# One-sided expert blocks of a mixture-of-experts kernel: the last weight chunk's low part is cast later, and the next block's column groups are turned in another order

## The chip, the cores and the metric

The kernel runs on one core of one Trainium2 chip. The metric is device time in microseconds (us) of one execution; three executions of the kernel before are shown. The core's engines are TensorE (PE; its weight loads are listed as PEld), VectorE (DVE), ScalarE (ACT), GpSimd (POOL) and SyncE (SP), and each runs its own list of instructions in order. They meet only where one waits for a count that another has reached.

## What is computed

Three stages on 1792 rows of width 768, in fp32:

```python
scores = scale * np.matmul(q, k.transpose(0, 1, 3, 2)) - np.log(S)   # 4 x 12 heads, 448 x 64
x = np.matmul(1.0 / (1.0 + np.exp(-scores)), v)                      # then one row per token, 768 wide

do_compute = x @ w_skip > 0                      # the other tokens keep x
e_idx = np.argmax(xc @ w_gate, axis=1)           # top-1 of 8 experts, xc = x[do_compute]
h = np.maximum(xc[mask] @ w1[e], 0.0)            # 768 -> 1024
out[do_compute] = xc + gate_w * (h @ w2[e])      # 1024 -> 768

h = out @ w_in                                   # dense, 768 -> 2048
g = np.where(h > 0.0, h, np.exp(np.minimum(h, 0.0)) - 1.0)
return g @ w_out                                 # 2048 -> 768
```

## The kernel before, in words

A product of two fp32 arrays is made of three matmuls on halves of the numbers: high by high, high by low, low by high (lines 556 to 558, `gemm`). So whatever enters a matmul is first cast to its **high part** by ACT and then has its **low part** (the value less its high part) made by DVE.

**Stages.** Attention comes first, then the experts, then the dense network. The change lies in the experts' stage, which ends 425.6 us after the start of the profiled span.

**Blocks.** The tokens that are not skipped are sorted by expert into blocks of 256 slots, two halves of 128 rows each; a block belongs to one expert. How many tokens an expert has is known only on the chip, so `level(i, k)` (line 1218) is a nest of branches that picks for block i one of several arms: both halves full, one half and a few rows, or the **one-sided arm**, one half only, `expert(i, k, (P,))`. In this run blocks 5, 6 and 7 are one-sided: they take 347 to 367.4, 367.4 to 388 and 388 to 408.4 us. There is no block 8 to compute; in its place `close(8)` and `after_close()` run, from 408.4 to 425.6 us, and turn the first rows of the dense stage.

**A one-sided block.** A block has 8 weight chunks of 128 x 1536, numbers 0 to 3 of w1 and 4 to 7 of w2. `split_w` casts a chunk's high part on ACT (line 547, tile `whi`) and makes its low part on DVE (line 549, tile `wlo`); there are 4 buffers of each. `ahead(i, c)` does so two chunks early, so that `ahead(i, 5)` makes the parts of **chunk 7**. In the one-sided arm the order of the program is: chunks 0 to 3 by `up_parts`, which leave h in rows (`hs`) in two halves; the first half of h turned into columns (`h_columns(0)`); `ahead(i, 5)` (line 1026); chunk 4 by `back`; the second half turned, `h_columns(1)`. A turn is four PE transposes (`flip`, line 142) into a PSUM bank, then ACT's relu of the bank to a high part (line 894) and DVE's low part (line 895). `h_columns(1)` uses bank `pt1`.

**Between two blocks.** The next level begins with `between(i)`: `columns(i, ends)` turns the next block's rows `xg` into columns, in three groups; each is four transposes by `flip_rows` (line 142 again) into one of the banks `ends = (pt0, pt1, acc1)`, then a high part by ACT (line 571) and a low part by DVE (line 573). Then come chunks 5 and 6 of the block before (`back`, lines 556 to 558), the branch `two` (line 1229), and chunk 7 of the block before in `lead_in`. `close` and `after_close` do the same at the end, with three more groups into other banks and a branch (line 1223) ahead of chunk 5.

**What sets the order.** Each engine's instructions stand in the order in which the program names them. An instruction that uses a tile waits for the tile's last users on other engines. It does so by a count: each engine counts its instructions up, and the wait names the count of the instruction that it needs. Two arms of one branch end at the same count, so that what follows can wait for a number that holds for both. `acc1`, the third of `ends`, is also the bank of a block's last product in the other two arms, where the last thing that DVE does is to add that product to the rows (`outcome`, line 1052).

Of the kernel before, what the change touches and what calls it, by code (L numbers as in the profile page):

```python
# [91 lines left out]
def build(nc, tc, a):  # L92
# [3 lines left out]
    with ExitStack() as top:  # L96
# [44 lines left out]
        def flip(dst, src):  # L141
            nc.tensor.transpose(dst, src, ident)  # L142
# [34 lines left out]
        with ExitStack() as st:  # L177
# [5 lines left out]
            x2 = both_t[:, : 2 * KD].rearrange("p (s c) n -> p s c n", s=2)  # L183
# [357 lines left out]
            def split_w(i, c, hi=True, lo=True):  # L541
                if i == NB:
                    return
                j = 8 * i + c
                raw, w_hi, w_lo = raw_of(i, c), whi_t[j % NSPL], wlo_t[j % NSPL]
                if hi:
                    nc.scalar.copy(w_hi, raw)  # L547
                if lo:
                    nc.vector.tensor_sub(w_lo, raw, w_hi)  # L549
# [10 lines left out]
            def flip_rows(i, g, pt):  # L560
                for j in range(2):
                    for h in range(2):
                        flip(
                            pt[:, (2 * j + h) * P : (2 * j + h + 1) * P],
                            xg_t[i % NXG][h][:, (2 * g + j) * P : (2 * g + j + 1) * P],
                        )

            def split_columns(g, pt, dst, hi=True, lo=True):
                o, pt = slice(2 * g, 2 * g + 2), pt.rearrange("p (c n) -> p c n", c=2)
                if hi:  # L570
                    nc.scalar.copy(dst[:, 0, o], pt)  # L571
                if lo:
                    nc.vector.tensor_sub(dst[:, 1, o], pt, dst[:, 0, o])  # L573

            def columns(i, banks):
                for g, pt in enumerate(banks):
                    flip_rows(i, g, pt)
                    split_columns(g, pt, x2)

            steps = B * NP  # L580
            raw = load(0, 0, True)
# [129 lines left out]
            ends = (*pt_t, acc_t[1])  # L711
# [167 lines left out]
            def h_columns(nh, sizes):  # L879
                for h, n in enumerate(sizes):  # L880
                    pt = pt_t[(nh + h) % 2].rearrange("p (c n) -> p c n", c=4)[:, :, :n]
                    for j in range(4):
                        w = slice(j * P, (j + 1) * P)
                        if n == P:
                            flip(pt[:, j, :], hs_t[nh][:, w])
                        else:
                            nc.tensor.matmul(
                                pt[:, j, :], hf_t[nh][:, w], fold[:, :n], start=True, stop=True
                            )
                    t = slice(h * P, h * P + n)  # L890
                    h_hi, h_lo = h2[:, nh, 0, :, t], h2[:, nh, 1, :, t]
                    if n < P:
                        h_lo = h2[:, nh, 0, :, h * P + n : (h + 1) * P]
                    nc.scalar.activation(h_hi, pt, AF.Relu)
                    nc.vector.scalar_tensor_tensor(
                        h_lo, pt, 0.0, h_hi, op0=ALU.max, op1=ALU.subtract
                    )
# [23 lines left out]
            def ahead(i, c, **parts):  # L921
                c += 2
                split_w(i + c // 8, c % 8, **parts)
# [87 lines left out]
            def expert(i, k, sizes, following=None):  # L1011
                whole = sizes == (P, P)

                def soon():
                    outcome(i - 1, 0, P)

                if whole:
                    up_two(i, soon)
                    ahead(i, 4)
                else:  # L1020
                    up_parts(i, sizes, soon)
                    if len(sizes) > 1:
                        skips(f"many{i}", 1 - (k >> 1))
                    elif i + 1 < NB:
                        skips(f"more{i + 1}", (following + 3) >> 2)
                ahead(i, 5)
                for h, n in list(enumerate(sizes))[1:]:
                    if whole:
                        back(i, h, n, range(4, 8))
                        outcome(i, h, n)  # L1030
                        back(i, 0, P, range(4, 5))
                    else:
                        back(i, h, n, range(4, 6))
                        h_columns(1, sizes)
                        back(i, h, n, range(6, 8))
                        back(i, 0, P, range(4, 5))
                        outcome(i, h, n)
                if len(sizes) == 1:
                    back(i, 0, P, range(4, 5))
                    h_columns(1, sizes)  # L1040

            def outcome(i, h, n):
                gated(xg_t[i % NXG][h], slot_gate[:, 2 * i + h : 2 * i + h + 1], h, n)
# [41 lines left out]
                    scatter(i - 2)  # L1085

            def between(i):
                columns(i, ends)
                back(i - 1, 0, P, range(5, 7))
                split_w(i, 0)  # L1090
                split_w(i, 1)
# [80 lines left out]
            def close(i):  # L1172
                if i == 1:
                    gather(1)
                s = 2 * (i - 1)
                nc.gpsimd.tensor_copy(last_rows[0], xg_t[(i - 1) % NXG][0])
                nc.gpsimd.tensor_copy(last_gate[0], slot_gate[:, s : s + 1])
                nc.gpsimd.tensor_copy(last_slot[0], slot_tok[:, s : s + 1])
                give(xg_t[(i - 1) % NXG][1], slot_tok[:, s + 1 : s + 2])
                for g in range(3):  # L1180
                    flip_rows(i, g, ends[g])
                for g in range(3):
                    flip_rows(i + 1, g, later[g])

            def after_close():

                for g in range(3):
                    split_columns(g, ends[g], x2)
                back(0, 0, P, range(5, 6))
                for g in range(3):  # L1190
                    split_columns(g, later[g], xd[:, 1], lo=g == 0)
                back(0, 0, P, range(6, 8))
                gated(last_rows[0], last_gate[0], 0, P)
                give(last_rows[0], last_slot[0])
                for g in range(1, 3):
                    split_columns(g, later[g], xd[:, 1], hi=False)
                xh, xl = x_dense
                terms = [(w[:, cc], xh[:, cc]) for w in wi0 for cc in range(KD)]
                terms += [(wi0[0][:, cc], xl[:, cc]) for cc in range(KD)]
                for k_, (w, x) in enumerate(terms):  # L1200
                    nc.tensor.matmul(  # L1201
                        acc_t[1], w, x, start=(k_ == 0), stop=(k_ == len(terms) - 1)
                    )
# [47 lines left out]
        with ExitStack() as st:  # L1251
# [156 lines left out]
            for s, (bi, f) in enumerate(steps):  # L1408
# [12 lines left out]
                g = curve(nt * P, ph)  # L1421
# [53 lines left out]
```

## Time and profile before

| | before |
|---|---|
| median of 3 executions | 904.13 us (903.27 to 906.42) |
| the profiled execution | 903.78 us |
| its span in the profile | 902.0 us |
| granted TensorE clock | 1.000 |
| PE busy | 880.9 us, 98% |
| DVE busy | 557.5 us, 62% |
| ACT busy | 485.5 us, 54% |

The profile shows one execution; its own time stands 0.35 us under the median, and the span 1.8 us under that, for what lies around it. Times in the trace count from the start of the span. A row of the timeline gives a start, a length and an instruction (or several alike in a row), and behind it in brackets how long the engine had been idle and on what it had waited. Matmuls overlap: one starts before the one ahead of it has ended.

### The profile page before, as it was taken

How to read it: one execution, taken by the hardware profiler on the slowest of the kernel's cores; microseconds unless marked ns; L12 is line 12 of the kernel's file. 1: busy time of each engine (PE TensorE's matmuls, PEld its weight loads, DVE VectorE, ACT ScalarE, POOL GpSimd, SP SyncE). 2: the span in 40 equal slices, each digit the busy share in tenths (PEclk: the TensorE clock that was granted, in tenths of full speed). 3: DMA queues.
4: the chain of work that ended last, by engine and by line, in shares of the span. 5: the costliest groups of instructions: out<-in, count | busy, mean ns of one | idle time of the engine just before them, and what ended most of it. 6: DMA issues, size and time to landing. Idle time of an engine off the chain costs nothing.

```text
span 902.0 us, 13626 instructions
## 1 busy us (share of the span) xinstructions
PE 880.9 (98%) x5208; PEld 710.4 (79%) x5208; DVE 557.5 (62%) x872; ACT 485.5 (54%) x680; POOL 80.8 (9%) x79
## 2 busy tenths in 40 slices
PE   9999999999999898998999999999999999999998
PEld 4445545699999787887888888888888888888997
DVE  2968778697666465885888886444344444344664
ACT  7777776554455464773645554434444434344664
POOL 1000000112101022332100000100000100000100
PEclk9999999999999999999999999999999999999999
DMA  8788875779956175955733430100000100000100
GB/s 291 260 281 274 302 262 200 262 276 405 373 181 232 45 293 202 410 215 197 242 96 102 123 105 19 70 1 18 18 18 19 70 1 1 1 1 18 53 1 36
DMA packets 34194, 134.71 MB, mean 149 GB/s; under 512 B 4698, under 2 KB 5850, under 8 KB 34098
## 3 DMA queue, kind: packets, MB, share of 16 engines
q1 hardware_dynamic: 29474, 114.22, 35.6%
q0 software_dynamic: 4480, 19.01, 5.9%
q8 instruction: 56, 0.92, 0.4%
q14 instruction: 40, 0.33, 0.1%
q10 hardware_dynamic: 144, 0.23, 0.1%
HBM read 112.47 MB, written 23.99 MB: 151 GB/s over the span
## 4 chain that ended last, share of the span: by engine, by line
PE 54%; issue 0%; DVE 0%; ACT 0%; ACTq 0%
PE acc L1350 16%; PE pt L1350 10%; PE acc L1318 9%; PE acc L1319 9%; PE acc L1317 8%; PE acc L142 1%; PE acc L1201 0%; PE acc L556 0%; PE acc L557 0%; PE acc L558 0%; DVE both L573 0%; ACT both L571 0%; ACT raw L1361 0%; ACTq L1471 0%; ACTq L571 0%
## 5 line engine op out<-in xcount | busy, mean ns | idle before, releaser
L549 DVE TENSOR_TENSOR wlo<-raw,whi 128x1536 fp32r<-128x1536 f32 x64 | 111.7, 1763 | 28.4 <-ACT whi L547 27.0
L1328 DVE SCALAR_TENSOR_TENSOR m<-m,acc 128x512 f32<-128x512 f32 (+1 forms) x64 | 39.7, 620 | 139.4 <-ACT m L1327 139.4
L1326 ACT ACTIVATE m<-acc 128x512 f32<-128x512 f32 (+1 forms) x64 | 34.9, 545 | 167.9 <-PE acc L1319 158.4
L547 ACT CAST whi<-raw 128x1536 fp32r<-128x1536 f32 x64 | 93.9, 1483 | 17.3 <-PE acc L558 6.6
L249 ACT ACTIVATE at<-ps,bias 112x896 f32<-112x896 f32 x96 | 88.9, 1010 | 23.3 <-PE ps L242 23.0
L1350 PE MATMUL acc<-wol,gh 128*128 128x256 f32 x320 | 100.8, 315 | 0.0
L1350 PE MATMUL acc<-woh,gl 128*128 128x256 f32 x320 | 100.4, 314 | 0.0
L1350 PE MATMUL acc<-woh,gh 128*128 128x256 f32 x320 | 100.4, 314 | 0.0
L1318 PE MATMUL acc<-x,wih 128*128 128x512 f32 (+1 forms) x270 | 96.2, 356 | 0.0
L1317 PE MATMUL acc<-x,wih 128*128 128x512 f32 (+1 forms) x270 | 96.2, 356 | 0.0
L1319 PE MATMUL acc<-x,wil 128*128 128x512 f32 (+1 forms) x270 | 96.1, 356 | 0.0
L556 PE MATMUL acc<-whi,both 128*128 128x384 f32 (+1 forms) x236 | 83.9, 355 | 2.7 <-DVE both L573 1.6
L557 PE MATMUL acc<-wlo,both 128*128 128x384 f32 (+1 forms) x236 | 82.9, 351 | 0.6 <-DVE wlo L549 0.6
L558 PE MATMUL acc<-whi,both 128*128 128x384 f32 (+1 forms) x236 | 82.5, 350 | 0.0
L256 PE MATMUL po<-at,vt 112*64 112x448 f32 x384 | 77.5, 545 | 0.0
L1306 DVE TENSOR_TENSOR wol<-wo,woh 128x768 fp32r<-128x768 f32 x64 | 61.2, 956 | 23.4 <-ACT woh L1305 23.0
L1350 PEld LDWEIGHTS acc<-woh,gh 128*128 128x128 f32 x320 | 60.3, 188 | 9.9
L1350 PEld LDWEIGHTS acc<-wol,gh 128*128 128x128 f32 x320 | 60.3, 188 | 9.5
L1305 ACT CAST woh<-wo 128x768 fp32r<-128x768 f32 x64 | 53.3, 833 | 26.0 <-PE acc L1350 25.9
L1332 DVE TENSOR_TENSOR gl<-m,gh 128x512 fp32r<-128x512 f32 (+1 forms) x64 | 40.0, 626 | 40.5 <-ACT gh L1331 40.5
L1350 PEld LDWEIGHTS acc<-woh,gl 128*128 128x128 f32 x320 | 60.1, 188 | 4.2
L1300 DVE TENSOR_TENSOR wil<-wi,wih 128x768 fp32r<-128x768 f32 x60 | 57.4, 956 | 7.6 <-ACT wih L1299 6.9
(268 smaller groups left out, 1872.2 us busy)
## 6 DMA issues: line engine op xcount, KB each, us to landing
raw<-in_w SPq DMA_DIRECT2D x66, 768.0 KB, 12.4
raw<-in_wi SPq DMA_DIRECT2D x9, 768.0 KB
raw<-in_wo SPq DMA_DIRECT2D x9, 768.0 KB, 7.1
vt<-in_v SPq DMA_DIRECT2D x12, 448.0 KB, 6.4
raw<-in_wi SPq DMA_DIRECT2D x14, 384.0 KB
raw<-in_wo SPq DMA_DIRECT2D x14, 384.0 KB, 3.1
qr<-in_q SPq DMA_DIRECT2D x11, 448.0 KB, 4.3
kr<-in_k SPq DMA_DIRECT2D x11, 448.0 KB, 4.1
```

Of the source, the lines that this page charges most:

```text
L249: nc.scalar.activation(at[:, :, c, :], ps[:CP, :, :S], AF.Sigmoid, bias=bias[:CP], scale=QK_SCALE)
L256: nc.tensor.matmul(po[64 * j : 64 * j + 64, :S], vt[:, 2 * (hp % 2) + j, c, :], at[:, j, c, :], start=(c == 0), stop=(c == NCH - 1),)
L547: nc.scalar.copy(w_hi, raw)
L549: nc.vector.tensor_sub(w_lo, raw, w_hi)
L556: nc.tensor.matmul(o, a_hi, b_hi, start=first, stop=False)
L557: nc.tensor.matmul(o, a_hi, b_lo, start=False, stop=False)
L558: nc.tensor.matmul(o, a_lo, b_hi, start=False, stop=last)
L1306: nc.vector.tensor_sub(pair[1], wo_r[f], pair[0])
L1317: nc.tensor.matmul(o, a, b, start=(cc == 0), stop=False)
L1318: nc.tensor.matmul(o, a, c, start=False, stop=False)
L1319: nc.tensor.matmul(o, wil[:, cc], b, start=False, stop=(cc == KD - 1))
L1350: nc.tensor.matmul(o, a, b, start=(clears and f == 0 and k_ == 0), stop=(f == KF2 - 1 and k_ == 2), skip_group_check=True,)
```

## The change

Two edits, both about the place where a one-sided block passes into the next one.

1. In the one-sided arm `ahead(i, 5)` makes only the high part of chunk 7 at its old place; the low part is made after `h_columns(1)`, so that on DVE it stands behind the low part of h's second half (line 895) and not ahead of it. The other arms keep both parts where they were.
2. `columns` takes an order of the groups, and `between`, `close` and `after_close` turn the groups first, third, second: the banks in the order `pt0`, `acc1`, `pt1`.

```diff
-            def columns(i, banks):
-                for g, pt in enumerate(banks):
-                    flip_rows(i, g, pt)
-                    split_columns(g, pt, x2)
+            def columns(i, banks, turns=(0, 1, 2)):
+                for g in turns:
+                    flip_rows(i, g, banks[g])
+                    split_columns(g, banks[g], x2)
...
-                ahead(i, 5)
+                ahead(i, 5, lo=len(sizes) > 1)
...
                 if len(sizes) == 1:
                     back(i, 0, P, range(4, 5))
                     h_columns(1, sizes)
+                    ahead(i, 5, hi=False)
...
             def between(i):
-                columns(i, ends)
+                columns(i, ends, (0, 2, 1))
...
-                for g in range(3):
+                for g in (0, 2, 1):
                     flip_rows(i, g, ends[g])
...
-                for g in range(3):
+                for g in (0, 2, 1):
                     split_columns(g, ends[g], x2)
```

From line 1039 on, the changed kernel's line numbers are one higher.

**On DVE**, at the end of a one-sided arm and the start of the next block (all these arms read alike): `wlo_1914` and `wlo_1916` are the low parts of chunks 6 and 7, `pt_1902` and `pt_1903` are `pt0` and `pt1`, and what stands in brackets is what the instruction waits for.

```order
 L895 SCALAR_TENSOR_TENSOR both<-pt_1902,both 128x4x128 [waits Activation_49]
 L549 TENSOR_TENSOR wlo_1914<-raw_2325,whi_1913 128x1536 [waits DMAHW2_49,Activation_49]
-L549 TENSOR_TENSOR wlo_1916<-raw_2326,whi_1915 128x1536 [waits DMAHW3_49,PE_49,Activation_49]
-L895 SCALAR_TENSOR_TENSOR both<-pt_1903,both 128x4x128 [waits Activation_49]
-L1229 UNCONDITIONAL_BRANCH
-L1223 COMPARE_AND_BRANCH
+L895 SCALAR_TENSOR_TENSOR both<-pt_1903,both 128x4x128 [waits Activation_49]
+L549 TENSOR_TENSOR wlo_1916<-raw_2326,whi_1915 128x1536 [waits DMAHW3_49,DVE_49]
+L1230 UNCONDITIONAL_BRANCH
+L1224 COMPARE_AND_BRANCH
 L573 TENSOR_TENSOR both<-pt_1902,both 128x512 [waits Activation_49]
```

The low part of chunk 7 and that of h have changed places, and the arm's last DVE instruction is now the former.

**On PE**, the same place in the kernel before: the last turn of h, the jump, and the first transpose into each of the three banks (`acc_1905` is `acc1`; `xg_1921` holds the next block's rows).

```order
L142 MATMUL pt_1903<-cst,hs_2317 128x128 [waits Activation_49]
L1229 UNCONDITIONAL_BRANCH
L1223 COMPARE_AND_BRANCH
L142 MATMUL pt_1902<-cst,xg_1921 128x128 [waits DMASW2_49,DVE_49]
...
L142 MATMUL pt_1903<-cst,xg_1921 128x128 [waits DVE_49]
...
L142 MATMUL acc_1905<-cst,xg_1921 128x128 [waits Activation_49]
...
L556 MATMUL acc_1908<-whi_1834,both 128x384
```

And in the changed kernel:

```order
L142 MATMUL pt_1903<-cst,hs_2317 128x128 [waits Activation_49]
L1230 UNCONDITIONAL_BRANCH
L1224 COMPARE_AND_BRANCH
L142 MATMUL pt_1902<-cst,xg_1921 128x128 [waits DMASW2_49,DVE_49]
...
L142 MATMUL acc_1905<-cst,xg_1921 128x128 [waits DVE_49,Activation_49]
...
L142 MATMUL pt_1903<-cst,xg_1921 128x128
...
L556 MATMUL acc_1908<-whi_1834,both 128x384
```

The transposes into `acc1` now stand second and carry a wait for DVE, and those into `pt1` stand third and carry none. In both built kernels the wait for DVE at this place asks for the count of the arm's last DVE instruction: behind block 5 that is 490, which before is line 895's and in the changed kernel that of chunk 7's low part.

## Rows read from the trace of the kernel before

**Rows 1.** The page: its span and the engines' busy time.

```profile
span 902.0 us, 13626 instructions
PE 880.9 (98%) x5208; PEld 710.4 (79%) x5208; DVE 557.5 (62%) x872; ACT 485.5 (54%) x680; POOL 80.8 (9%) x79
```

**Rows 2.** Windows: from:to and length, each engine's busy time, PE's clock, DMA share, GB/s.

```profile
core 0: us, PE busy (x) PEld busy (x) DVE busy (x) ACT busy (x) POOL busy (x), PEclk, DMA share, GB/s
408.40:425.60 17.20, 14.00 (x85) 12.71 (x84) 8.52 (x12) 4.68 (x9) 4.07 (x4) 1.00 0.67 226
425.60:850.00 424.40, 424.36 (x2210) 360.27 (x2209) 233.65 (x381) 198.66 (x323) 20.17 (x20) 1.00 0.16 53
```

**Rows 3.** Timeline of PE where block 5 passes into block 6.

```profile
start us, us, engine line op out<-in xcount [idle before <-releaser]
367.47 0.60 PE L142 MATMUL pt<-cst,hs 128*128 128x128 f32 x4
367.90 0.60 PE L142 MATMUL pt<-cst,xg 128*128 128x128 f32 x4
370.00 0.66 PE L142 MATMUL pt<-cst,xg 128*128 128x128 f32 x4 [1.50 <-DVE both L895]
370.50 0.60 PE L142 MATMUL acc<-cst,xg 128*128 128x128 f32 x4
370.85 0.42 PE L556 MATMUL acc<-whi,both 128*128 128x384 f32 x1
375.09 0.34 PE L556 MATMUL acc<-whi,both 128*128 128x384 f32 x1
```

**Rows 4.** Timeline of DVE at the same place.

```profile
367.59 1.76 DVE L549 TENSOR_TENSOR wlo<-raw,whi 128x1536 fp32r<-128x1536 f32 x1 [0.32 <-ACT whi L547]
369.26 0.68 DVE L895 SCALAR_TENSOR_TENSOR both<-pt,both 128x512 fp32r<-128x512 f32 x1
369.86 0.68 DVE L573 TENSOR_TENSOR both<-pt,both 128x512 fp32r<-128x512 f32 x1
```

**Rows 5.** Timeline of ACT at the same place.

```profile
366.08 1.48 ACT L547 CAST whi<-raw 128x1536 fp32r<-128x1536 f32 x1
368.11 0.60 ACT L894 ACTIVATE both<-pt 128x512 fp32r<-128x512 f32 x1 [0.55 <-PE pt L142]
368.60 0.58 ACT L571 CAST both<-pt 128x512 fp32r<-128x512 f32 x1
```

**Rows 6.** Timeline of PE behind block 6 (first row) and at the close.

```profile
390.49 0.66 PE L142 MATMUL pt<-cst,xg 128*128 128x128 f32 x4 [1.51 <-DVE both L895]
...
408.44 0.60 PE L142 MATMUL pt<-cst,hs 128*128 128x128 f32 x4
...
411.10 0.66 PE L142 MATMUL pt<-cst,xg 128*128 128x128 f32 x4 [1.63 <-DVE both L895]
411.60 1.91 PE L142 MATMUL acc<-cst,xg 128*128 128x128 f32 x16
415.07 0.41 PE L556 MATMUL acc<-whi,both 128*128 128x384 f32 x1 [1.57 <-DVE both L573]
```

**Rows 7.** Timeline of DVE (both parts in one row), then ACT, at the close.

```profile
406.48 3.96 DVE L549 TENSOR_TENSOR wlo<-raw,whi 128x1536 fp32r<-128x1536 f32 x2
410.37 0.68 DVE L895 SCALAR_TENSOR_TENSOR both<-pt,both 128x512 fp32r<-128x512 f32 x1
...
409.07 0.60 ACT L894 ACTIVATE both<-pt 128x512 fp32r<-128x512 f32 x1 [0.55 <-PE pt L142]
```

**Rows 8.** Timeline of PE and DVE where block 4 passes into block 5.

```profile
347.63 1.09 PE L142 MATMUL pt<-cst,xg 128*128 128x128 f32 x8 [0.98 <-DVE rest L1216]
...
347.42 0.15 DVE L1216 COPY rest<-cst 128x1 f32<-128x1 f32 x1
```

**Rows 9.** Lines 1206 and 1223 by PE's sequencer: count, shortest/median/longest ns, starts.

```profile
L1206 PEldq TENSOR_LOAD <-kinds x1: 307/307/307, 372.0 to 372.0; - x1
...
L1223 PEldq EVENT_SEMAPHORE  x1: 51/51/51, 411.4 to 411.4; - x1
L1223 PEldq COMPARE_BRANCH  x1: 3303/3303/3303, 411.6 to 411.6; - x1
```

**Rows 10.** Line 1229 by PE's sequencer in blocks 5 and 6; PE's timeline in block 5.

```profile
L1229 PEldq COMPARE_BRANCH  x1: 3028/3028/3028, 351.4 to 351.4; - x1
...
L1229 PEldq COMPARE_BRANCH  x1: 447/447/447, 372.4 to 372.4; - x1
...
354.50 0.45 PE L556 MATMUL acc<-whi,both 128*128 128x384 f32 x1 [1.18 <-issue]
```

## The prediction

> **What bounds the kernel now.** I read the page first: PE is busy for 880.9 of 902.0 us [rows 1], so a change counts for as much as it moves PE's idle time, or PE's work. The change has neither more nor fewer instructions of any kind; it can only move idle time. The windows come next: from 425.6 to 850 us PE is busy for 424.36 of 424.40 us [rows 2]. What the experts' stage loses is therefore not made up later: the dense stage has no idle time that could shrink, and a loss passes to the end whole. The window of the close has 17.20 − 14.00 = 3.2 us of idle PE [rows 2].
>
> Then PE's timeline where a one-sided block passes into the next. Behind block 5 it turns h's second half at 367.47, the next block's first group into `pt0` at 367.90, and then stands idle for 1.50 us, till line 895 on DVE has emptied `pt1` [rows 3]. DVE's timeline says why that was late: ACT's relu of `pt1` had ended at 368.11 + 0.60 = 368.71 [rows 5], but DVE was on chunk 7's low part from 367.59, and took line 895 only at 369.26, till 369.94 [rows 4]. PE's idle time ends 0.06 us later, at 370.00. The same is to be seen behind block 6 (1.51 us) and at the close (1.63 us) [rows 6]. These three gaps, 4.6 us together, are all that the change can touch: at the other boundaries no one-sided arm ends.
>
> **What the change aims at.** Line 895 would start when ACT's relu ends, at 368.71 + 0.03 = 368.74 (estimated delay; rows 4 and 5 show no case of their own), and end at 369.42, which is 0.52 us earlier. PE would spend the wait on the transposes into `acc1`. If these need not wait, the gap shrinks.
>
> **What I take them to wait for.** They do wait. The order of the changed kernel shows that the first transpose into `acc1` carries a wait for DVE, where before it had none of its own: it stood behind `pt1`'s, which asked for the same count. That count is the last of the arm, since in the other arms `acc1`'s last reader on DVE is the arm's last instruction, and all arms end at one count. In the kernel before, the one-sided arm's last instruction on DVE is line 895, so that the wait asked for no more than `pt1` needed. In the changed kernel the last is the low part of chunk 7, which no transpose needs. So PE waits in second place for **the very instruction that was moved out of line 895's way**.
>
> Does such a wait for unrelated work bind on the chip? Between blocks 4 and 5 it does: the transposes into `pt0` started at 347.63, idle for 0.98 us, when a DVE copy that only fills up the arm's count (line 1216, which nobody reads) had ended at 347.42 + 0.15 = 347.57 [rows 8].
>
> **The two inner boundaries** (5 to 6, 6 to 7), by block 5's rows. Line 895 runs from 368.74. The next instruction on DVE starts 0.60 us after it, as 369.86 after 369.26 [rows 4]: chunk 7's low part starts at 369.34 and ends, at 1.76 us [rows 4], at 371.10. Its high part was ready at 366.08 + 1.48 = 367.56 [rows 5], so it waits for nothing else. 0.06 us later, at 371.16, PE turns `acc1`'s group, against 370.00 for the first of the two groups before: 1.16 us more idle time. The wait now stands as an instruction of its own in PE's sequencer instead of on the transpose, so the restart has an empty queue; I add an estimated 0.04 us (0 to 0.1). **1.2 us each, 2.4 together** (2.3 to 2.5).
>
> What follows: ACT's cast of `pt0` was done at 368.60 + 0.58 [rows 5] and waits for nobody; DVE's subtraction of it comes 1.2 us later than 369.86 and is needed only by the next block's first chunk, which comes after chunk 7, itself at 375.09 before [rows 3] and now at 376.3. Chunk 7's low part, done at 371.10, is 5 us early for it. So neither ACT nor DVE is late next. The branch between chunks 6 and 7 was met by the sequencer at 372.4 and took 0.45 us [rows 10], 2.2 us ahead of chunk 7: that is the cover, and it stays about as long, as both move. The DMAs and their queues (SP, POOL) keep their places; the low part reads a buffer that is reloaded much later, and 1.2 us do not show there.
>
> **The close** has the same wait and a branch behind it. The relu ends at 409.07 + 0.60 = 409.67 [rows 7]; line 895 would start at 409.70, the low part at 410.30 and end at 412.06, and PE would go on at 412.12 in place of 411.10 [rows 6]: 1.0 us. Then comes what PE's sequencer does. Before, it had handed on 19 transposes during the idle time and came to the branch 0.3 us after the release (its wait at 411.4), and the branch took it 3.303 us [rows 9]: 411.6 + 3.3 = 414.9, and chunk 5 started at 415.07 [rows 6]. So the branch sets chunk 5's start, not the transposes, which ended at 413.5. The changed kernel's sequencer is held at the wait, and then has 20 transposes to hand on before it meets the branch. Behind block 5 it was, at 372.0, past 8 transposes and 24 matmuls [rows 9], when PE had started 8 and 7 of them (24 matmuls from 370.85 to 375.09 [rows 3] are one in 0.177 us): 17 ahead. With 17 ahead it meets the branch when PE begins the fourth transpose, 0.4 us after the release in place of 0.3: the close costs 1.0 + 0.1 = 1.1 us. If it can't get ahead, 20 transposes at 0.12 us each (16 in 1.91 [rows 6]) make 2.4 us: 1.0 + 2.4 − 0.3 = 3.1 us. I take **1.5**, near the lower end, because of the 17.
>
> **The sum.** 1.2 + 1.2 + 1.5 = 3.9 us (2.3 + 1.1 = 3.4 to 2.5 + 3.1 = 5.6). The sum stands against the profiled execution's 903.78 us: 907.7. That execution lies 0.35 us under the median of 904.13, which is well inside the three runs' spread of 3 us. About 0.3% of 904.13, 2.7 us, is what a measurement of this kernel can tell from no change; 3.9 is 0.4%. The case's own range: 906.5 to 909.5.
>
> **Rivals.**
>
> *The wait is over sooner (a gain).* If the transposes into `acc1` are held only until line 895, or not at all, the change does what its parts look like. Not at all: `acc1`'s group fills the idle time and `pt1`'s starts at 369.42 + 0.06 = 369.48, where before the first of the two started at 370.00: with one group done already, PE's next chunk comes 0.52 + 0.35 (a group's time before chunk 5, 370.50 to 370.85 [rows 3]) = 0.87 us earlier; twice, and about 1.0 at the close (1.63 [rows 6] less what is left of it): 2.7 us in all, so 901.1. For it: line 895 does come earlier. Against: the count in the built kernel, and the copy of rows 8. It decides if DVE's count stands otherwise than I read it. 0.05.
>
> *The close hides its share.* If chunk 5's start at 415.07 is set by something that does not move with the wait, only the inner boundaries count: 903.78 + 2.4 = 906.2, within 0.3%. For it: the profile puts that idle time down to line 573 on DVE [rows 6], and the transposes would end at 412.12 + 0.5 + 1.9 = 414.5, still ahead of 415.07. Against: chunk 5 reads nothing of line 573's, and the branch ends 0.16 us ahead of it. The Trainium skill ("Advanced Engine Details and Errata", section "Control Flow Timing") gives a compare-and-branch about 108 ns; by that the branch could not have held chunk 5, and this rival would be the forecast. The 3.303 us of rows 9 speak against it here, thirty times as long. 0.14.
>
> *A slow branch at the inner boundaries too.* In block 5 the branch between chunks 6 and 7 took 3.028 us and left PE idle for 1.18 us [rows 10]; behind it 0.447. With the sequencer held till 371.2 and then 17 ahead, it meets the branch at about 373.2; at 3.03 us it is through at 376.2, and PE's chunk 7, due at 376.3, comes up to 0.4 us later: 3.9 + 2 × 0.4 = 4.7, 908.5. For it: one of three such branches was slow. Against: what is fetched does not change with a microsecond of delay. 0.08.
>
> *Nothing changes*: the waits trade places and times as they were, 903.8 to 904.1. That needs line 895 and the low part to run as before, which their order excludes. 0.03.
>
> **How the numbers follow.** Forecast 0.70, gain 0.05, hidden close 0.14, slow branch 0.08, nothing 0.03. Faster by over 0.3%: the gain case, 0.05 (its 901.1 lies just at that bound; I count it whole). Within 0.3% (up to 906.8): the hidden close, nothing, and some 0.03 of the forecast's lower edge: 0.20. Slower: 0.75. The forecast is 907.7; the range goes down to 905.8, for a hidden close, and up to 909.8, for a close at PE's pace with a little of the slow branch.
>
> **What would show it.** In the changed profile PE's timeline behind blocks 5 and 6 should show one idle time of about 2.7 us (1.50 + 1.2) ahead of the transposes into `acc` rather than `pt`, ended by line 549, not 895, and no idle time ahead of `pt1`'s. On DVE line 895 should start 0.03 us after line 894 ends, and the low part 0.60 us later. At the close the wait of line 1224 should be met at about 412.6 (plus the 2.4 us by which all has moved) and chunk 5 come 3.9 us later than 415.07. I am wrong if the transposes into `acc1` start before the low part ends; if they do wait but chunk 5 at the close comes only 2.4 us later, the second rival holds.

## The result and the profile after

The changed kernel took **911.01 us** in the median of 5 executions (909.07 to 912.09), the kernel before 903.76 (902.89 to 906.42): a ratio of 1.0068, 95% interval [1.0047, 1.0088] (ratios, here and below, are taken over the single executions and need not be the quotient of the medians). It is slower, as forecast, but by about 7 us in place of 3.9, and the median lies outside the range of 905.8 to 909.8. The profiled execution was the fastest of the five, 909.07 us with a span of 907.3; its mean granted clock was 0.995, where that of before was 1.000.

PE's timeline of the changed kernel where block 5 passes into block 6, which answers to [rows 3]:

```profile
367.46 0.60 PE L142 MATMUL pt<-cst,hs 128*128 128x128 f32 x4
367.89 0.60 PE L142 MATMUL pt<-cst,xg 128*128 128x128 f32 x4
371.23 0.63 PE L142 MATMUL acc<-cst,xg 128*128 128x128 f32 x4 [2.73 <-DVE wlo L549]
371.69 0.60 PE L142 MATMUL pt<-cst,xg 128*128 128x128 f32 x4
372.04 0.42 PE L556 MATMUL acc<-whi,both 128*128 128x384 f32 x1
372.30 0.33 PE L557 MATMUL acc<-wlo,both 128*128 128x384 f32 x1
...
372.97 0.52 PE L557 MATMUL acc<-wlo,both 128*128 128x384 f32 x1
373.29 0.52 PE L558 MATMUL acc<-whi,both 128*128 128x384 f32 x1
...
376.46 0.34 PE L557 MATMUL acc<-wlo,both 128*128 128x384 f32 x1
376.64 0.34 PE L558 MATMUL acc<-whi,both 128*128 128x384 f32 x1
```

The first four rows are the forecast: the idle time stands ahead of `acc1`'s transposes, is 2.73 us long (1.50 + 1.23) and is ended by line 549. The rows behind them are not in the forecast: from 372.65 to 375.85 the matmuls of chunks 5 and 6 follow each other at 0.32 us, then again at 0.17. DVE at the same place, for [rows 4]:

```profile
368.72 0.69 DVE L895 SCALAR_TENSOR_TENSOR both<-pt,both 128x512 fp32r<-128x512 f32 x1 [1.47 <-ACT both L894]
369.33 1.75 DVE L549 TENSOR_TENSOR wlo<-raw,whi 128x1536 fp32r<-128x1536 f32 x1
```

Line 895 starts at 368.72 (forecast 368.74), the low part at 369.33 (369.34), and it ends at 371.08. The waits of the whole span, and the windows of the stretches that matter (columns as in [rows 2]):

```profile
PE acc L142 <- DVE wlo L549: 8.2, 3, 2.7
```

```profile
372.50:376.00 3.50, 3.50 (x13) 3.50 (x12) 2.92 (x3) 2.02 (x3) 0.86 (x1) 0.52 1.03 419
372.80:375.60 2.80, 2.80 (x11) 2.80 (x10) 2.23 (x3) 1.53 (x2) 0.46 (x1) 0.50 1.02 418
390.70:412.40 21.70, 18.97 (x106) 17.15 (x105) 18.08 (x15) 15.34 (x16) 9.19 (x7) 1.00 0.26 87
412.40:420.20 7.80, 4.74 (x29) 4.16 (x28) 4.24 (x5) 2.24 (x5) 1.00 (x1) 0.79 0.34 98
```

Windows of the kernel before, behind its idle times of 1.50 and 1.51 us:

```profile
370.00:375.00 5.00, 5.00 (x32) 5.00 (x33) 3.66 (x5) 3.93 (x4) 0.00 (x0) 1.00 1.01 414
390.50:395.50 5.00, 5.00 (x32) 5.00 (x33) 3.65 (x5) 3.94 (x4) 0.00 (x0) 1.00 0.51 200
```

The three idle times make 8.2 us, where before they made 4.6 [rows 3, 6]. And **the granted clock is 0.50 behind the first of them**: TensorE runs at 1.2 GHz in place of 2.4, with PE busy all the time. Behind the second it stays at 1.00. Behind the third, at the close, it falls again (0.79 in the mean of that window). (The Trainium skill, "TensorE: Matmul & The Clock Gate", section "What's actually happening", knows no other levels than these two; the 0.50 of the window agrees.)

The close, for [rows 6, 9]:

```profile
416.16 0.63 PE L142 MATMUL acc<-cst,xg 128*128 128x128 f32 x4 [2.73 <-DVE wlo L549]
...
417.11 2.77 PE L142 MATMUL acc<-cst,xg 128*128 128x128 f32 x12
420.20 0.52 PE L556 MATMUL acc<-whi,both 128*128 128x384 f32 x1 [0.33 <-issue]
```

```profile
L1224 PEldq EVENT_SEMAPHORE  x1: 51/51/51, 416.4 to 416.4; - x1
L1224 PEldq COMPARE_BRANCH  x1: 3467/3467/3467, 416.6 to 416.6; - x1
```

The sequencer met the branch's wait 0.24 us after the release, and the branch took 3.467 us; it ended 0.13 us ahead of chunk 5 (before, 0.17 us). The twelve transposes at the lower clock (2.77 us, where sixteen had taken 1.91) are hidden behind it.

**Where the time went.** PE's timeline gives four pieces: from the last turn of h in block 5 to that in block 6, on to that at the close, on to chunk 5 there, and on to the end of the span. Before: 387.94 − 367.47 = 20.47; 20.50; 6.63; 902.0 − 415.07 = 486.93. The table has for each kernel of this study the difference to these, worked out in the same way from its own timeline, and the place where block 5's last turn begins.

| profiled execution | begins | block 6 | block 7 | close | rest |
|---|---|---|---|---|---|
| before | 367.47 | 20.47 | 20.50 | 6.63 | 486.93 |
| changed | 367.46 | +2.77 | +1.19 | +1.18 | +0.17 |
| changed, again | 368.59 | +2.67 | +2.79 | +1.47 | +1.65 |
| `order_only` | 368.12 | +0.08 | +0.05 | +0.34 | −0.02 |
| `lo_only` | 368.06 | +0.78 | +0.78 | +0.92 | +1.63 |
| `lo_out` | 369.83 | −0.44 | −0.47 | −0.44 | +0.09 |
| `free_bank` | 368.07 | −0.95 | −0.97 | +0.90 | +1.32 |
| `fill` | 377.91 | +1.21 | +1.19 | +1.51 | −0.05 |
| `gap_1024` | 366.95 | +2.53 | +2.87 | +1.37 | +0.05 |
| `gap_512` | 367.05 | +2.30 | +0.71 | +1.01 | +1.70 |
| before, again | 367.96 | +0.01 | −0.02 | +0.72 | +1.50 |
| `before_c5` | 369.32 | −0.75 | −0.79 | +0.28 | +0.01 |
| `after_c5` | 372.52 | +0.09 | +0.07 | +1.63 | +1.56 |
| `lo_between` | 368.60 | −0.95 | −0.97 | −0.33 | −0.08 |

For the changed kernel the four make 5.3, the whole difference of the spans (907.3 − 902.0). The place where block 5's last turn begins differs by 1.1 us between the two profiles of the changed kernel, and most of that is there long before the experts: attention's products behind an idle time of 0.87 us start at 12.88 us in the one and at 13.60 in the other. That is why the pieces tell more than the times.

### The profile page after: what moved, and what is told of

Same layout as the page of the kernel before. It is cut to its first block, busy times and chain, and to the rows that moved or that the text cites. A ratio compares the mean times of both kernels' runs of the same rounds, so it can differ in the third digit from the quotient of the medians.

```text
span 907.3 us, 13633 instructions
## 1 busy us (share of the span) xinstructions
PE 883.6 (97%) x5208; PEld 713.3 (79%) x5208; DVE 557.4 (61%) x872; ACT 485.2 (53%) x680; POOL 78.6 (9%) x79
## 4 chain that ended last, share of the span: by engine, by line
PE 91%; DVE 4%; DMA 2%; issue 1%; ACT 1%; SPq 0%; POOL 0%; DVEq 0%; ACTq 0%
PE acc L1351 16%; PE pt L1351 10%; PE acc L1320 8%; PE acc L1319 8%; PE acc L1318 8%; PE po L256 7%; PE ps L242 6%; PE acc L556 6%; PE acc L557 5%; PE acc L558 5%; DVE wlo L549 2%; PE acc L142 2%; PE acc L916 1%; PE acc L917 1%; PE pt L142 1%
```

## Experiments

Two questions: is it the count of the arm's last DVE instruction that PE waits for, and what lowers the clock? All ratios are to the kernel before on the same chip, in the same session.

### The wait: each edit by itself

`lo_only` has the first edit alone (against the kernel before):

```diff
-                ahead(i, 5)
+                ahead(i, 5, lo=len(sizes) > 1)
...
                     h_columns(1, sizes)
+                    ahead(i, 5, hi=False)
```

> The first edit alone: chunk 7's low part behind line 895, groups in the old order pt0, pt1, acc1. Theory: pt1's transposes wait for line 895 alone and start 1.6 us after those into pt0 have started (369.48 in the time of the kernel before), acc1's wait for the low part and start where they do in the changed kernel, 3.8 us after the last turn of h: idle time in two pieces of about 1.0 and 1.2 us. Chunk 5 comes 0.35 us sooner than in the changed kernel and 0.8 later than before: 903.8 + 2 x 0.8 + 0.7 = 906.1 (905.3 to 906.8), and the clock, with no idle time over 1.5 us, stays at 1.000. Rival A (the clock falls with any second wait, or for another reason): 908 to 911.

Measured: 909.27 us, ratio 1.0056 [1.0038, 1.0074]. The inner boundary is as expected; PE's timeline:

```profile
370.07 0.66 PE L142 MATMUL pt<-cst,xg 128*128 128x128 f32 x4 [0.98 <-DVE both L895]
371.82 0.63 PE L142 MATMUL acc<-cst,xg 128*128 128x128 f32 x4 [1.10 <-DVE wlo L549]
...
418.14 0.41 PE L556 MATMUL acc<-whi,both 128*128 128x384 f32 x1 [1.84 <-DVE both L573]
```

`pt1` waits for line 895, and `acc1`, here third as in the kernel before, for the low part, which reads nothing from that bank. The clock stays up behind both inner boundaries (+0.78 each, expected 0.8). But behind the 1.84 us of the close it falls, and the rest of the span is 1.63 us longer; this I had not expected. It is half of the 3 us by which the time is over the forecast; of the other half, 0.7 us is what the profiled execution (908.53 us) lies under the median, which no profile shows, and the rest is a later start and 0.2 us more at the close.

`order_only` has the second edit alone.

```diff
-                columns(i, ends)
+                columns(i, ends, (0, 2, 1))
```

> The second edit alone: the order pt0, acc1, pt1, with chunk 7's low part where it was before. Theory: the arm's last DVE instruction is line 895, as before; acc1's transposes start where pt1's did (370.00 in the time of the kernel before), pt1's behind them; idle times of 1.50 us as before and no fall of the clock there: 903.8 to 904.5, no difference from the kernel before (within 0.15%). Rival C (the order itself costs): 906 or more.

Measured: 906.02, ratio 1.0016 [1.0001, 1.0031], where no more than 0.15% was expected. The order alone costs 0.08 and 0.05 us: `acc1` waits for line 895 and starts 2.63 us after the last turn of h, where `pt1` in the kernel before started 2.53 us after it. Line 895 ends at 370.60 here, 0.15 us ahead of the transposes, against 0.06 us before: the 0.1 us is what a wait of its own in PE's sequencer (here at 370.6) costs over one on the transpose. The median is at the 906 that rival C gave, but the profile places no more than 0.5 us at the three boundaries (the close is 0.34 longer); 0.65 us is a later start, and the rest is not placed.

```profile
368.12 0.60 PE L142 MATMUL pt<-cst,hs 128*128 128x128 f32 x4
...
370.75 0.63 PE L142 MATMUL acc<-cst,xg 128*128 128x128 f32 x4 [1.59 <-DVE both L895]
```

`lo_out` leaves PE's order and waits as the change has them, and makes the low part elsewhere (against the changed kernel; likewise in `close`):

```diff
-                ahead(i, 5, lo=len(sizes) > 1)
+                ahead(i, 5, lo=False)
...
-                    ahead(i, 5, hi=False)
...
                 columns(i, ends, (0, 2, 1))
+                if i > 1:
+                    ahead(i - 1, 5, hi=False)
```

> The changed kernel with chunk 7's low part taken out of every arm of expert and made in between, behind the three column groups (and in close). PE's order and its waits stand as in the changed kernel, acc1 second and waiting for the count of the arm's last DVE instruction; but in the one-sided arm that is line 895 again. Theory (the count is what costs): PE goes on 0.06 us after line 895, 2.0 us after the last turn of h, idle 1.0 us in place of 2.73 at all three places, no fall of the clock there; chunk 5 comes 0.5 us sooner than in the kernel before: 903.8 - 1.5 = 902.3 (901.3 to 904), clock 0.998 or more. Rival C (the order acc1 ahead of pt1 is what costs, or the wait's form): idle 2.7 us and 909 to 912. Rival E (the low part comes too late for chunk 7, or delays the next block's first low parts): idle time ended by line 549 ahead of line 557, 904 to 907.

Measured: 905.35, ratio 1.0002 [0.9987, 1.0016], no difference from before. PE's timeline:

```profile
251.35 0.36 PE L556 MATMUL acc<-both,whi 128*128 128x256 f32 x1 [0.66 <-DVE rest L1220]
...
371.94 0.63 PE L142 MATMUL acc<-cst,xg 128*128 128x128 f32 x4 [1.07 <-DVE both L895]
```

This is the run that shows the count. The same transposes, second in order, with the same form of wait, stand idle for 1.07 us and not 2.73, since the arm's last DVE instruction is line 895 again. All three pieces are some 0.45 us shorter than before, as expected; yet the time is not. The edit reaches the other arms too, and one of the waits that it brought there is the 0.66 us ahead of 251.35, which the kernel before does not have (rival E, at another place than I had put it). From the transposes at 170.71, ahead of the first block, to a matmul of line 916 in block 3 at 306.56 this profile takes 1.9 us more than the kernel before (169.99 to 303.96); the other 1.2 us of that are not placed, and 0.7 us is a later start.

`free_bank` is the changed kernel with another bank:

```diff
-            ends = (*pt_t, acc_t[1])
-            later = (acc_t[3], acc_t[5], acc_t[0])
+            ends = (*pt_t, acc_t[5])
+            later = (acc_t[1], acc_t[3], acc_t[0])
```

> The changed kernel with the third group's bank acc5, whose last reader is in the block before, in place of acc1 (and acc1, acc3, acc0 for the three later groups of the close). Theory: the transposes into acc5 wait for nothing and fill the idle time, pt1's wait for line 895 and start at 369.48 in the time of the kernel before: 0.87 us gained at each inner boundary, about 0.9 at the close: 903.8 - 2.6 = 901.2 (900.4 to 902.2), clock 1.000. Rival C (the wait is not the count of the arm's last instruction but the order itself, or the low part delays something else on DVE): 906 to 911.

Measured: 902.98, ratio 0.9982 [0.9968, 0.9996]: a little faster than before, less than expected.

```profile
368.94 0.60 PE L142 MATMUL acc<-cst,xg 128*128 128x128 f32 x4
370.08 0.66 PE L142 MATMUL pt<-cst,xg 128*128 128x128 f32 x4 [0.54 <-DVE both L895]
...
410.84 1.50 PE L142 MATMUL acc<-cst,xg 128*128 128x128 f32 x12 [1.05 <-ACTq L1224]
414.65 0.66 PE L556 MATMUL acc<-whi,both 128*128 128x384 f32 x1 [2.31 <-DVE both L573]
```

At the inner boundaries 0.95 and 0.97 us are gained (expected 0.87): the bank without the late wait gives what the change seems to be for. At the close I had overlooked that `acc1` now stands first among the later groups and brings its wait along: 1.05 us idle (the row names ACT's branch, but PE's sequencer was in a wait till 410.75, and the low part on DVE ended at 410.74), then 2.31 behind the branch, at the lower clock in the rest.

### The clock

`fill` gives PE something to do in the idle time (against the changed kernel; what it multiplies goes nowhere):

```diff
                     ahead(i, 5, hi=False)
+                    for j in range(10):
+                        nc.tensor.matmul(acc_t[5], iota_h,
+                            one_hot[0][:, 4 * (j % 3) : 4 * (j % 3) + 4], start=True, stop=True)
```

> The changed kernel, with ten matmuls of 128x512 into the unused bank acc5 behind the last turn of h in every one-sided arm; their result is read by nobody. Theory (the idle time of 2.73 us is the wait for chunk 7's low part, and TensorE's clock falls behind it): the wait ends as before, 3.8 us after the start of the last turn of h, so the stalls keep their 3.5 us, but PE is at work for some 2.1 us of it and the clock stays at 1.000: 903.8 + 3.5 = 907.3 (906.5 to 908.3). Rival A (the fall of the clock has nothing to do with the idle time): as the changed kernel, 911, clock 0.992 to 0.996. Rival B (the profile's view of the clock is right, but it costs no time): also 911.

Measured: 918.11, ratio 1.0158 [1.0131, 1.0186]: slower by far, and the forecast time is a miss. Block 5's last turn of h begins 10.4 us later than before, ahead of all that the edit meant to touch: PE is idle for 3.29 us ahead of block 5's first transposes, and the branch `two` there took 6.347 us where it had been 3.028 [rows 10]. That the added code is the reason, by moving what lies behind it, is likely but was not tried by itself.

```profile
352.02 1.09 PE L142 MATMUL pt<-cst,xg 128*128 128x128 f32 x4 [3.29 <-issue]
...
363.38 0.44 PE L556 MATMUL acc<-whi,both 128*128 128x384 f32 x1 [3.24 <-issue]
...
377.91 0.60 PE L142 MATMUL pt<-cst,hs 128*128 128x128 f32 x4
378.35 2.32 PE L1043 MATMUL acc<-one_hot,iota_h 128*128 128x512 f16 x10
...
381.68 0.63 PE L142 MATMUL acc<-cst,xg 128*128 128x128 f32 x4 [0.57 <-DVE wlo L549]
```

```profile
352.00:356.00 4.00, 3.98 (x17) 4.00 (x18) 1.91 (x3) 2.32 (x4) 0.00 (x0) 0.50 1.02 408
363.00:367.00 4.00, 3.62 (x13) 3.62 (x14) 1.16 (x2) 0.00 (x0) 0.00 (x0) 0.63 1.03 401
377.90:399.60 21.70, 21.13 (x116) 18.17 (x115) 18.02 (x15) 15.46 (x16) 3.93 (x3) 1.00 0.89 305
399.60:421.30 21.70, 21.13 (x116) 18.17 (x115) 18.17 (x15) 15.47 (x16) 9.48 (x7) 1.00 0.20 65
```

At the two boundaries themselves it says what it was made for. `acc1` still starts 3.77 us after the last turn of h (381.68 − 377.91, as 371.23 − 367.46), so the wait is whole; but PE is idle for only 0.57 us of it, the clock is 1.00 through both blocks, and they take 21.68 and 21.69 us: what the changed kernel's block 7 took without a fall, and 1.5 us less than its block 6 with one. The four pieces make 3.9 us, where 3.5 were forecast. And behind the two idle times of over 3 us in block 5 the clock fell.

`gap_1024` and `gap_512` lengthen the idle time of the kernel before, in its own order:

```diff
                 ahead(i, 5)
+                if len(sizes) == 1:
+                    raw, (w_hi, w_lo) = raw_of(i, 7), weights(i, 7)
+                    nc.vector.tensor_sub(w_lo[:, :1024], raw[:, :1024], w_hi[:, :1024])
```

> The kernel before, in its own order of everything, with 1024 of the 1536 columns of chunk 7's low part made twice in a one-sided arm, so that line 895 comes some 1.17 us later: idle time 1.50 + 1.17 = 2.67 us ahead of the transposes into pt1. Theory: the stalls cost 3 x 1.17 = 3.5 us and the clock falls behind some of them, at 1.5 us each, as in the changed kernel: 909 to 912, with a stretch at about 0.54 behind block 5 or 6. Rival A (the fall belongs to the changed order, or to that session): 907.3 with the clock at 1.000.

> The kernel before, in its own order, with 512 of the 1536 columns of chunk 7's low part made twice: line 895 0.6 us later, idle time 1.50 + 0.6 = 2.1 us, halfway to the changed kernel's 2.73. If the clock does not fall behind 2.1 us: 3 x 0.6 = 1.8, 905.6 (904.8 to 906.4), clock 1.000. If it falls as behind 2.73 us: 907 to 910, with stretches at the lower clock behind block 5 or 6.

Measured: 910.16, ratio 1.0072 [1.0051, 1.0092], for 1024 columns; 907.19, ratio 1.0034 [1.0017, 1.0050], for 512. PE's timeline and the windows of the first:

```profile
370.74 1.12 PE L142 MATMUL pt<-cst,xg 128*128 128x128 f32 x4 [2.76 <-DVE both L895]
...
393.75 0.98 PE L142 MATMUL pt<-cst,xg 128*128 128x128 f32 x4 [2.77 <-DVE both L895]
```

```profile
370.70:374.20 3.50, 3.46 (x16) 3.46 (x17) 1.97 (x3) 2.04 (x3) 0.00 (x0) 0.61 1.01 420
394.00:398.00 4.00, 4.00 (x18) 4.00 (x17) 2.06 (x4) 2.54 (x3) 2.16 (x3) 0.58 0.26 71
```

and of the second:

```profile
370.31 0.66 PE L142 MATMUL pt<-cst,xg 128*128 128x128 f32 x4 [2.22 <-DVE both L895]
...
393.08 0.66 PE L142 MATMUL pt<-cst,xg 128*128 128x128 f32 x4 [2.22 <-DVE both L895]
```

```profile
371.00:374.00 3.00, 3.00 (x13) 3.00 (x12) 1.81 (x3) 2.44 (x3) 0.00 (x0) 0.54 1.02 422
394.00:398.00 4.00, 4.00 (x25) 4.00 (x24) 3.03 (x4) 3.71 (x4) 1.01 (x1) 1.00 0.14 50
```

With neither of the change's two edits, a longer idle time alone gives the changed kernel's time and its lower clock. At 2.22 us it fell behind one of two equal idle times: block 6 took 2.30 us more, block 7 0.71, so that this fall cost 1.6.

The changed kernel and the kernel before, each once more:

> The changed kernel once more, beside the next three on one chip. Theory (three waits of 2.73 us for the low part, 3.5 us in all over the kernel before, and on top 1.5 us for each time that the clock falls behind one, which need not be at the same boundaries in every execution): 907.3 to 912, idle times of 2.73 us as before, the stretches at the lower clock behind other ones of the three or behind more of them than in the first profile. Rival D (the clock's share is fixed by the program): the same one stretch behind block 5 and one at the close.

> The kernel before once more, for a second profile. Theory: idle times of 1.50, 1.51 and 1.63 us at the three places and the clock at 1.000 behind the two inner ones, as in the first profile, whatever the time of this execution (901.5 to 907.7). Rival D (the clock falls at random, not by the length of the idle time): a stretch at the lower clock behind block 5 or 6.

Measured: the changed kernel 911.07, ratio 1.0074 [1.0054, 1.0093], its profiled execution the slowest, 913.52; the kernel before 906.54, one execution. The changed kernel's timeline at the two inner boundaries, and its windows:

```profile
372.36 1.09 PE L142 MATMUL acc<-cst,xg 128*128 128x128 f32 x4 [2.73 <-DVE wlo L549]
...
395.50 0.71 PE L142 MATMUL acc<-cst,xg 128*128 128x128 f32 x4 [2.73 <-DVE wlo L549]
```

```profile
372.40:376.00 3.60, 3.60 (x16) 3.60 (x17) 1.80 (x3) 2.25 (x3) 0.05 (x1) 0.58 1.03 424
395.60:399.40 3.80, 3.80 (x17) 3.80 (x18) 2.05 (x4) 2.54 (x3) 2.63 (x3) 0.55 0.60 149
422.00:426.00 4.00, 3.22 (x11) 2.91 (x10) 0.00 (x0) 0.59 (x1) 0.00 (x0) 0.50 0.97 332
```

The idle times are 2.73 us as in the first profile, but now the clock falls behind both inner ones, and at the close late enough to slow the chunks behind the branch (+1.65 in the rest). The fall is not fixed by the program. In the kernel before both inner idle times were 1.50 us, and the clock held there; at the close chunk 5 was idle for 2.19 us this time, where it had been 1.57 [rows 6], and the clock fell behind it, which is 1.5 of that execution's 2.7 us more.

### A better version

`before_c5` and `after_c5` put a real piece of work into the idle time, chunk 5, between the first and the second turn (in `between` alone; `before_c5` is shown, and `after_c5` does the same with the groups in the order 0, 2, 1):

```diff
-                columns(i, ends)
-                back(i - 1, 0, P, range(5, 7))
+                for g in (0, 1, 2):
+                    flip_rows(i, g, ends[g])
+                    split_columns(g, ends[g], x2)
+                    if g == 0:
+                        back(i - 1, 0, P, range(5, 6))
+                back(i - 1, 0, P, range(6, 7))
```

> The kernel before with chunk 5 of the block before between the first and the second group's turn, in between alone. Theory: line 895 ends while PE is on chunk 5 (which waits for ACT's line 894, 0.4 us); no idle time over 0.5 us is left at the two inner boundaries and chunk 6 comes 1.2 us sooner at each: 903.8 - 2.4 = 901.4 (900.4 to 902.6). Rival E (the columns of the next block come too late when their turns stand behind chunk 5, there and between the other blocks): 904 or more, with idle time ahead of the next block's first chunk.

> The changed kernel with chunk 5 of the block before put between the first and the second group's turn, at the inner boundaries alone: the same instructions in another order on PE, which works for 2.1 us of the idle time. The close is left as in the changed kernel. Theory: the transposes into acc1 still wait for the low part (3.8 us after the last turn of h), with 0.3 to 0.5 us of idle time left; chunk 6 comes 0.9 us sooner than in the kernel before at both boundaries; the clock stays at full speed there; the close costs 1.2 us as in the changed kernel, and up to 1.5 for its clock: 903.8 - 1.7 + 1.2 = 903.3 (902.5 to 905). Rival A (the fall of the clock does not come from the idle time): a stretch at the lower clock behind block 5 or 6 all the same, 905 to 908.

Measured: 906.19, ratio 1.0022 [1.0006, 1.0038], and 912.57, ratio 1.0087 [1.0063, 1.0112]. Both miss. The idle time at the inner boundaries is gone in the first (block 6 is 0.75 us shorter, 1.2 expected); in the second 0.65 us of it is left, with the clock up there, and block 6 is no shorter than before; but `between` serves every arm, and elsewhere PE now waits, as in these rows of `before_c5`, neither of which the kernel before has:

```profile
215.25 0.36 PE L556 MATMUL acc<-both,whi 128*128 128x256 f32 x1 [1.54 <-DVE rest L1220]
...
387.20 0.44 PE L558 MATMUL acc<-whi,both 128*128 128x384 f32 x1 [0.68 <-DVE both L895]
```

The first comes twice in each of the two kernels, the second three times in `before_c5` and twice in `after_c5`. `after_c5` loses the most: besides these waits, its clock fell ahead of block 4, behind 1.92 us of idle time, and at the close, behind 2.12 us, for some 1.5 us each.

`lo_between` has both cures of the wait, `lo_out` and `free_bank` together (of each place only the added lines are shown, and `ahead(i, 5, lo=False)` and `close` are left out).

```diff
+            ends = (*pt_t, acc_t[5])
+            later = (acc_t[1], acc_t[3], acc_t[0])
...
                 columns(i, ends, (0, 2, 1))
+                if i > 1:
+                    ahead(i - 1, 5, hi=False)
```

> Both cures together: chunk 7's low part in between behind the column groups, as in the run beside this, and acc5 as the second group's bank, which waits for nothing (acc1, acc3, acc0 for the close's later groups). Theory: PE idle for 0.54 us at all three places, chunk 5 0.95 us sooner than before at the two inner boundaries, and at the close, where acc1 now waits for line 895's count alone, the branch is met 0.6 us sooner than before: 903.8 - 2.5 = 901.3 (900.3 to 903). Rival E (the low part comes too late at chunk 7, or the blocks before, whose arms have the same edit, lose time): 903 to 906.

Measured: 903.00, ratio 0.9979 [0.9961, 0.9997]. It is 0.2% faster than the kernel before, less than the forecast 2.5 us; with `free_bank`, from which it can't be told apart, it is the fastest kernel of the study. Both inner blocks are 0.95 and 0.97 us shorter than before, and its close 0.33, with the 0.54 us of idle time that were expected at all three places. What is missing in the profiled execution lies ahead of block 5: there the clock fell behind an idle time of 2.04 us, and the way from a matmul of line 916 in block 3 at 304.89 to the like one in block 4 at 342.72 took 1.56 us more than before (303.96 to 340.23). The six executions with a mean clock of 1.000 took 899.1 to 903.3 us, the six with 0.998, of which this is one, 902.7 to 905.4.

## Why the prediction was wrong

**Right: what PE waits for.** The count of the arm's last DVE instruction holds `acc1`'s transposes until the low part is done. `lo_out` takes this one thing away and the wait goes with it; `free_bank` takes the bank with that count away, and 0.95 us are gained. The rival of a gain (0.05) fell, and so did that of no change.

**Right: the price of the wait.** Forecast 1.2 us for each inner boundary; measured 2.73 − 1.50 = 1.23 and 2.73 − 1.51 = 1.22, and +1.19 for block 7, where nothing else happened. The close, taken as 1.5 within 1.1 to 3.1, was 1.18 in the first profile: the sequencer met the branch 0.24 us after the release, even earlier than with the 17 instructions that I had let it run ahead. The hidden close (0.14) is out: chunk 5 moved with the branch, which took 3.467 us. That is again far from the 108 ns that the Trainium skill's page "Advanced Engine Details and Errata", section "Control Flow Timing", gives. The slow branch at the inner boundaries (0.08) did come, so the reason given against it does not hold: line 1230 took 3.303 and 1.192 us there, where it had been 0.447 and 0.448. But it stayed covered. Block 7's +1.19 has no room for it, and in block 6 it ended at 377.3, ahead of chunk 7 at 377.85; chunk 7 was late there by the slower pace told next, so whether 3.3 us would have shown at the full pace is open. The 0.04 us that the estimate put on a wait of its own was 0.09 (the low part ends at 371.08, PE goes on at 371.23, against 0.06 before).

**Wrong: the sum.** It is in the step that follows the wait ("So neither ACT nor DVE is late next"): the prediction asked what is late behind the longer idle time, and not whether PE works at the same pace behind it. 24 matmuls at 0.177 us were carried over from [rows 3] into the changed kernel. There ten of them ran at 0.32: 10 × 0.15 = 1.5 us, and block 6's +2.77 is the wait's 1.23 and this. The term was missing from the forecast and from both ends of the range. The profile of before could not show it, since its clock stood at 1.00 behind idle times of 1.5 us (the two windows of the kernel before, above); the prediction should have said that no row of before had 2.7 us of idle time with PE's pace behind it at these places, and kept a bound for it.

With it the times come out: without a fall 903.8 + 1.23 + 1.19 + 1.18 = 907.4, within 0.3 us of the forecast; with one inner fall of 1.5 us 908.9, which the first profile has (909.07); with two and a late one at the close, 907.4 + 1.4 + 1.6 + 0.3 + 1.65 = 912.4, and the second profile's 913.52 began its block 6 1.1 us later. That the other executions, 909.9 to 912.1, differ by their number of falls is argued from these two, not shown: they have no profile, only mean clocks of 0.992 to 0.996, and these do not put them in order (911.01 us came with 0.996, 909.07 with 0.995). Of the 7 us between the medians, 5.3 are placed by the first profile; the other 2 are open.

**Open.** Why the clock falls behind one of two equal idle times and not the other was not tried.

## What to carry to other kernels

Before an instruction is moved to the end of an arm, look who waits for the arm's count: in this kernel the last instruction on DVE was waited for by whoever shares a tile with another arm's last one, needed or not. A wait on TensorE can cost twice, once for its length and once for the pace of what follows it: at the inner boundaries the pace fell behind six of eight idle times of 2.2 to 2.8 us. And a move that is meant for one arm should not pass through code that all arms share.

## What was not expected of the hardware

The clock behind an idle time at the two inner boundaries, and in block 5 of `fill`, by the profiles of this study (`before_c5` and `after_c5`, which move chunk 5 into that place, are left out; `lo_only` has two idle times at each boundary, counted as one case):

| idle time of PE | cases | clock fell to 1.2 GHz behind it |
|---|---|---|
| 0.54 to 1.10 us (`free_bank`, `lo_out`, `lo_only`, `lo_between`, `fill`) | 10 | 0 |
| 1.50 to 1.60 (before twice, `order_only`) | 6 | 0 |
| 2.22 (`gap_512`) | 2 | 1 |
| 2.73 (changed twice) | 4 | 3 |
| 2.76, 2.77 (`gap_1024`) | 2 | 2 |
| 3.24, 3.29 (`fill`, block 5) | 2 | 2 |

A fall cost 1.3 to 1.6 us at these boundaries, more than the lengthened wait itself (1.23). The length alone does not decide. Elsewhere the clock fell behind 1.84 us (`lo_only`, at the close, with another idle time shortly ahead) and, ahead of block 4, behind 1.92 us (`after_c5`) and 2.04 us (`lo_between`); it did not fall behind 2.05 us (the kernel before) and 2.24 us (`fill`) at that same place, nor behind 2.33 us at the close of `lo_between`.

The branch `two` in block 5 took 2.8 to 3.2 us in nine of the fourteen profiles, 1.1 to 2.6 in four, and 6.3 in `fill`, which has ten matmuls more in each one-sided arm. That code added in one place is paid for in another is what this suggests; no run tried it by itself.
